# Placing the work around chunks 1 to 3 anew in a fused attention and maxout feed-forward kernel

## The chip, the cores and the metric

The kernel runs on one core of one Trainium2 chip. The core has a matrix engine (TensorE, PE in the profile, with its weight loads as PEld), a vector engine (VectorE, DVE), a scalar engine (ScalarE, ACT), a general engine (GpSimd, POOL) and a queue engine (SyncE, SP) that mostly issues transfers. Each engine runs its own list of instructions in order and waits on semaphores for the others. The metric is the device time of one execution, in microseconds (us).

## The reference: what is computed

Attention with a sliding window of 128 keys and 4 sink keys, for 4 batches of 8 heads, 768 positions and a head dimension of 64. Its result, taken as 3072 tokens of 512 features, then goes through a feed-forward layer whose hidden activation is the largest of three products.

```python
scores = scale * np.matmul(q, k.transpose(0, 1, 3, 2))
keep = is_sink | in_window            # first 4 keys, or 0 <= i - j < 128
a = softmax(np.where(keep, scores, -1e9))
x = np.matmul(a, v)                   # as [3072, 512]
h = np.maximum(np.maximum(x @ w1, x @ w2), x @ w3)   # [3072, 768]
out = h @ w_out                       # [3072, 512], float32
```

## The kernel before

**Tiling.** The 3072 tokens are cut into 12 chunks of 256 tokens, three to a batch (`ci // 3` is the batch, `ci % 3` the place in it). For each chunk the kernel makes these steps, each a small function:

- `load(ci, 'kqv')` issues the transfers of the raw float32 Q, K and V (SP's queue). A `gate` is a tiny POOL instruction that writes into the target first, so that the transfer waits for it.
- `cast_qk(ci, w, g, eng)` makes bf16 of half of Q or K (`g` is the group: head pairs 0 and 1, or 2 and 3), and `cast_v(ci, n, i, eng)` of a quarter of V, on the engine named.
- `turn(ci, w, g, eng)` brings the head dimension onto the partitions: four PE transposes into a PSUM bank, and a copy out of it by `eng`. From chunk 4 on `turn_dma` does that with a transposing transfer from SP's queue instead.
- `score(ci, (p,))` multiplies Q and K of head pair `p` (tile `st`, L331), `expo` takes the exponential on ACT (L398), and `mask` zeroes what is outside the window on DVE (L406). `sink_score` does it for the sink keys (tile `sk`).
- `av_open(ci)` takes four PSUM banks for the output of the four pairs (tile `o`) and, in chunks that have sinks apart, adds the sinks' share (L453). `av(ci, p)` adds the window's share (L471), then `norm` divides on DVE (L481 and L484, into `x_sb`).
- `xpose(ci, t, eng)` transposes a half of the result on PE and copies it into `xT`; from chunk 3 on `xpose_dma(ci)` does it with one transposing transfer (L503).
- `ffn_h(ci, fp, wi)` is one piece of the hidden layer: eight matmuls for a third of the columns (`fp`) with weight matrix `wi` (tile `h_ps`, L524). For `wi` = 0 ACT copies it to `h_sb` (L536); for 1 and 2 DVE takes the maximum into `h_sb` (L540). Nine pieces make a chunk.
- `ffn_y(ci, t)` is the output product for half of the tokens of a chunk: six matmuls (tile `y_ps`, L553), then a copy (L555).

**Order.** Nothing is scheduled by a tool: under `tc.manual_schedule()` every engine runs its instructions in the order in which the Python code calls them. So a line that is moved in the list at the end of the function moves its instructions on every engine that they touch. Chunks 0 to 3 are written out by hand, since the weights still arrive there; from chunk 4 on a loop repeats one order.

**Banks.** PSUM has eight banks, which `bank()` hands out by a first-in, first-out list, and `give()` puts back. A matmul into a bank waits until the instruction that last read the bank has finished. So the order of the calls also decides which earlier copy, exponential or maximum each matmul waits for.

**Buffers.** Raw Q, K and V have two buffers each (`bufs=2`), the turned tiles `qT`, `kT` and the V tiles `vb` a ring of four (`RING = 4`): chunk 4 uses the tiles of chunk 0. `kT_69` to `kT_72`, `qT_73` to `qT_76` and `vb_77` to `vb_80` are the ring's tiles 0 to 3 in the listings.

Of the kernel before, what the change touches and what calls it, by code (L numbers as in the profile page):

```python
# [16 lines left out]
def kernel(  # L17
# [13 lines left out]
    nc = tc.nc  # L31
# [17 lines left out]
    with tc.manual_schedule():  # L49
# [13 lines left out]
        def give(*banks):  # L63
            for x in banks:
                free.append(home.pop(id(x))[1])
# [46 lines left out]
        def cast_qk(ci, w, g, eng):  # L112

            if (ci, w) not in bfs:
                bfs[ci, w] = raw.tile([128, NP, 2, 2, D], BF16, tag=w + "_bf", name=w + "_bf")
            x, y = bfs[ci, w], raws[ci, w]
            f = eng.copy if eng is nc.scalar else eng.tensor_copy
            f(x[:, 2 * g:2 * g + 2].rearrange("q p i a d -> q p a i d"),  # L118
              y[:, 4 * g:4 * g + 4].rearrange("q (p a) i d -> q p a i d", a=2))

        def cast_v(ci, n, i, eng):
            if ci < NEW:
                eng.tensor_copy(  # L123
                    vb[ci % RING][64 * i:64 * i + 64, n, :, 0:D],
                    raws[ci, "v"][64 * n:64 * n + 64, :, i])
                return
            for h in range(2):
                x, y = 64 * h + 32 * i, 64 * n + 32 * h
                eng.tensor_copy(  # L129
                    vb[ci % RING][x:x + 32, n, :, 0:D], raws[ci, "v"][y:y + 32, :, i])  # L130
# [261 lines left out]
        def expo(ci, p):  # L392
            if ci >= NEW:
                return expo4(ci, p)
            lo = 0 if ci % CPB else 1
            e, st = es[ci, p]
            for a in range(2):
                nc.scalar.activation(e[:, a, lo:], st[a][:, lo:], AF.Exp, scale=scale)  # L398
                give(st[a])

        def mask(ci, p, eng=None):
            if ci >= NEW:
                return mask4(ci, p)
            lo = 0 if ci % CPB else 1
            e = es[ci, p][0]
            (eng or nc.vector).tensor_mul(e[:, :, lo:], e[:, :, lo:], msk0[0] if lo else msk)  # L406
# [38 lines left out]
        def av_open(ci):  # L445
            b, c = divmod(ci, CPB)
            for p in range(NP):
                os_[ci, p] = bank([128, 2, 2, D + 1], F32, "o")
            if c:
                for t in range(2):  # L450
                    for p in range(NP):
                        hp = slice(32 * p, 32 * p + 32)
                        nc.tensor.matmul(  # L453
                            os_[ci, p][:, t], lhsT=es[ci, "sink"][hp, t], rhs=vs[b % 2][hp],
                            start=(t == 0), stop=False, skip_group_check=True,
                            tile_position=(32 * p, 0))
# [54 lines left out]
        def ffn_h(ci, fp, wi, cuts=1, eng=nc.scalar, then=True):  # L511
            if ci not in hs:
                hs[ci] = work.tile([128, FB, 256], BF16, tag="h", bufs=3, name="h_sb")
            hp = bank([128, 2, 256], F32, "h_ps")
            for f in range(2):
                c0 = (2 * fp + f) * 128
                for ds in range(DS):
                    x = xTs[ci][:, ds]
                    if ci < NEW:
                        x = x.rearrange("q t (i r) -> q i t r", i=2)  # L520
                    else:
                        x = (x.rearrange("q t c -> q (t c)")
                             .rearrange("q (j i r) -> q i j r", i=2, r=32))
                    nc.tensor.matmul(  # L524
                        hp[:, f].rearrange("q (i t r) -> q i t r", i=2, r=x.shape[3]),
                        lhsT=w_sb[wi][:, ds, c0:c0 + 128], rhs=x,
                        start=(ds == 0), stop=(ds == DS - 1))
            maxima[ci, fp, wi] = hp
            if then:
                ffn_max(ci, fp, wi, cuts, eng)  # L530
# [14 lines left out]
        def ffn_y(ci, t, eng=None):  # L545
            if t == 0 and ci == 0:
                y01 = work.tile([128, 2, 2, d_model], F32, tag="y01", bufs=1, name="y01_sb")
                ys[0], ys[1], ys["01"] = y01[:, 0], y01[:, 1], y01
            if t == 0 and ci > 1:
                ys[ci] = work.tile([128, 2, d_model], F32, tag="y", bufs=5, name="y_sb")  # L550
            yp = bank([128, d_model], F32, "y_ps")
            for fb in range(FB):
                nc.tensor.matmul(yp, lhsT=hs[ci][:, fb, t * 128:(t + 1) * 128], rhs=wo[:, fb],  # L553
                                 start=(fb == 0), stop=(fb == FB - 1))
            (nc.scalar.copy if eng is None else eng.tensor_copy)(ys[ci][:, t], yp)  # L555
            give(yp)
# [197 lines left out]
        ffn_h(1, 1, 1)  # L754
        turn(2, 'k', 1, nc.scalar)
        cast_qk(2, 'q', 1, nc.scalar)
        cast_qk(2, 'q', 0, nc.vector)
        ffn_h(1, 2, 1)
        ffn_h(1, 1, 2)
        ffn_h(0, 0, 2)  # L760
        turn(2, 'q', 1, nc.scalar)
        ffn_h(0, 1, 2)
# [12 lines left out]
        cast_v(2, 1, 0, nc.gpsimd)  # L775
        cast_v(2, 0, 0, nc.gpsimd)
        ffn_h(0, 2, 2)
        ffn_h(1, 2, 2)
        score(2, (2,))
        cast_qk(3, 'q', 0, nc.gpsimd)  # L780
        av_open(2)
        mask(2, 1)
        expo(2, 2)
        cast_qk(3, 'k', 0, nc.gpsimd)
        load(4, 'v')
        mask(2, 3)
        mask(2, 2)
        cast_v(2, 1, 1, nc.vector)
        cast_v(2, 0, 1, nc.vector)
        cast_qk(3, 'q', 1, nc.vector)  # L790
        ffn_y(0, 0)
        ffn_y(0, 1)
        ffn_y(1, 0)
        av(2, 0)
        turn(3, 'q', 0, nc.scalar)
        cast_qk(3, 'k', 1, nc.scalar)
        load(5, 'q')
        av(2, 2)
        load(5, 'k', gate=after(0, 300))
        av(2, 3)  # L800
        turn(3, 'q', 1, nc.scalar)
        av(2, 1)
        turn(3, 'k', 1, nc.scalar)
        turn(3, 'k', 0, nc.scalar)
        ffn_y(1, 1)
        xpose(2, 0, nc.scalar)
        xpose(2, 1, nc.vector)
        cast_qk(4, 'q', 1, nc.vector)
        cast_v(3, 0, 0, nc.gpsimd)
        cast_v(3, 0, 1, nc.gpsimd)  # L810
        score(3, (1,))
        cast_v(3, 1, 1, nc.gpsimd)
        cast_qk(4, 'q', 0, nc.vector)
        expo(3, 1)
        score(3, (0,))
        cast_qk(4, 'k', 0, nc.vector)
        cast_qk(4, 'k', 1, nc.gpsimd)
        mask(3, 1)
        score(3, (3,))
        ffn_h(2, 0, 0)  # L820
        cast_v(4, 1, 0, nc.gpsimd)
        cast_v(3, 1, 0, nc.vector)
        turn_dma(4, 'k')
        turn_dma(4, 'q')
        expo(3, 0)
        expo(3, 3)
        score(3, (2,))
        ffn_h(2, 0, 2)
        mask(3, 0)
        mask(3, 3)  # L830
        ffn_h(2, 1, 0)
        ffn_h(2, 0, 1)
        expo(3, 2)
        av_open(3)
        mask(3, 2)
        av(3, 0)
        av(3, 1)
        ffn_h(2, 1, 1)
        av(3, 3)
        ffn_h(2, 2, 0)  # L840
# [158 lines left out]
```

## Time and profile before

| what | value |
|---|---|
| median of 3 runs | 177.17 us (176.39 to 177.6) |
| the profiled execution's own time | 176.99 us |
| its span, from first to last instruction | 175.3 us |
| PE busy | 168.9 us (96%) |
| DVE / POOL / ACT busy | 126.9 / 108.4 / 89.0 us |
| mean granted TensorE clock | 0.997 |
| from HBM / to HBM | 25.17 / 6.29 MB |

The span is 1.7 us shorter than the time of the same execution; the rest lies around it. Busy time of PE is modelled, and matmuls overlap: a PE that is shown busy can still be waiting inside a matmul, which is then seen as a longer distance from one start to the next. "[0.27 <-ACT k_bf L118]" behind a row says how long the engine sat idle before it, and what ended that. A piece of the chain of work that ended last reads "start, duration, what".

### The profile page before, as it was taken

The page shows a single profiled execution, that of the slowest core. Times are in us where ns is not written, and L with a number is a line of the kernel's source. Part 1 is how long each engine was busy: PE and PEld are TensorE (multiplying, and loading weights), DVE is VectorE, ACT ScalarE, POOL GpSimd, SP SyncE. Part 2 cuts the span into 40 slices and gives each one's busy share as a digit, 9 for nine tenths or more (in the row PEclk, how much of TensorE's full clock was granted, in tenths as well). Part 3 has the DMA queues.
Part 4 walks back from the last instruction along what each step waited for, and adds up shares of the span by engine and source line. Part 5 has one row for each costly group of instructions (what it writes and reads, how often), then busy time and mean ns, then how long its engine had stood idle before and what let it go on. Part 6 is the DMA issues. An engine that isn't in the chain of part 4 may idle for free.

```text
span 175.3 us, 5418 instructions
## 1 busy us (share of the span) xinstructions
PE 168.9 (96%) x2225; PEld 129.8 (74%) x2225; DVE 126.9 (72%) x264; ACT 89.0 (51%) x183; POOL 108.4 (62%) x191
## 2 busy tenths in 40 slices
PE   7979999999999999999999999999999999999992
PEld 2546899756687588698797797797797797796871
DVE  3177854799699797787976985986877777776452
ACT  4498654586863822925817717717726616510210
POOL 7389507244589999999999999789997700000000
PEclk9999999999999999999999999999999999999998
DMA  5999999999998997996999998998999509118303
GB/s 144 300 285 197 215 217 174 235 304 288 288 212 193 171 251 149 234 246 174 245 202 254 259 194 221 262 187 211 257 182 279 38 17 361 49 25 278 122 0 120
DMA packets 71545, 35.22 MB, mean 201 GB/s; under 512 B 27488, under 2 KB 69984, under 8 KB 71520
## 3 DMA queue, kind: packets, MB, share of 16 engines
q1 hardware_dynamic: 65824, 31.60, 76.9%
q0 software_dynamic: 5552, 3.15, 13.0%
q8 instruction: 17, 0.28, 0.7%
q10 hardware_dynamic: 144, 0.13, 0.2%
q14 instruction: 8, 0.07, 0.1%
HBM read 25.17 MB, written 6.29 MB: 179 GB/s over the span
## 4 chain that ended last, share of the span: by engine, by line
PE 87%; DVE 4%; ACT 3%; DMA 3%; issue 1%; ACTq 0%
PE h_ps L524 53%; PE y_ps L577 11%; PE o L471 6%; PE y_ps L553 5%; PE st L357 3%; PE warm L203 3%; DMA xT<-x_sb 3%; ACT e_sb L398 2%; PE pt L138 2%; PE st L331 1%; DVE vb L123 1%; PE o L453 1%; DVE x_sb L484 1%; PE y_ps L599 1%; PE sk L423 1%
## 5 line engine op out<-in xcount | busy, mean ns | idle before, releaser
L524 PE MATMUL h_ps<-xT,w 128*128 128x256 bf16 x864 | 101.2, 273 | 0.2
L524 PEld LDWEIGHTS <-w 128*128 128x128 bf16 x864 | 81.9, 98 | 10.3 <-DMA xT<-x_sb 0.5
L540 DVE TENSOR_TENSOR h_sb<-h_sb,h_ps 128x512 bf16<-128x512 bf16 (+1 forms) x74 | 49.0, 671 | 19.3 <-PE h_ps L524 15.6
L536 ACT CAST h_sb<-h_ps 128x512 bf16<-128x512 f32 x35 | 20.5, 586 | 52.6 <-PE h_ps L524 52.6
L129 POOL CAST vb<-v_raw 32x512 bf16<-32x512 f32 x48 | 37.0, 770 | 3.2 <-DMA v_raw<-in_v_dram 1.0
L90 POOL CAST k_bf<-k_raw 32x512 bf16<-32x512 f32 x48 | 29.1, 607 | 3.4 <-DMA k_raw<-in_k_dram 1.3
L398 ACT ACTIVATE e_sb<-st 128x512 bf16<-128x512 f32 (+1 forms) x48 | 23.1, 586 | 0.8 <-PE st L331 0.7
L484 DVE TENSOR_TENSOR x_sb<-o,rc 128x256 bf16<-128x256 f32 x48 | 20.4, 425 | 1.7
L577 PE MATMUL y_ps<-wo,h_sb 64*64 64x512 bf16 (+1 forms) x312 | 21.1, 377 | 0.0
L471 PE MATMUL o<-vb,e_sb 128*128 128x65 bf16 x352 | 16.8, 194 | 0.4 <-DVE vb L123 0.4
L471 PEld LDWEIGHTS <-e_sb 128*128 128x128 bf16 x352 | 14.6, 97 | 2.9 <-issue 0.8
L406 DVE TENSOR_TENSOR e_sb<-e_sb,msk 128x1024 bf16<-128x1024 bf16 (+1 forms) x18 | 15.3, 869 | 1.7 <-ACT e_sb L398 1.6
L123 POOL CAST vb<-v_raw 64x512 bf16<-64x512 f32 x16 | 11.4, 713 | 7.4 <-DMA v_raw<-in_v_dram 6.9
L389 DVE TENSOR_TENSOR e_sb<-e_part,msk 128x1024 bf16<-128x1024 bf16 x16 | 13.1, 831 | 3.3 <-ACT e_part L374 3.1
L577 PEld LDWEIGHTS <-h_sb 64*64 64x64 bf16 (+1 forms) x312 | 9.9, 106 | 5.0
L374 ACT ACTIVATE e_part<-st 128x384 bf16<-128x384 f32 x32 | 13.1, 496 | 0.5 <-PE st L357 0.5
L553 PE MATMUL y_ps<-wo,h_sb 128*128 128x512 bf16 x54 | 12.8, 380 | 0.0
L481 DVE RECIPROCAL rc<-o 128x4 f32<-128x4 f32 x48 | 8.4, 175 | 3.3 <-PE o L471 3.1
L118 POOL CAST k_bf<-k_raw 128x512 bf16<-128x512 f32 x6 | 4.1, 694 | 9.9 <-DMA k_raw<-in_k_dram 9.8
L553 PEld LDWEIGHTS <-h_sb 128*128 128x128 bf16 x54 | 4.9, 98 | 5.8 <-DVE h_sb L540 1.0
L118 ACT CAST q_bf<-q_raw 128x512 bf16<-128x512 f32 x13 | 7.6, 621 | 1.8 <-DMA q_raw<-in_q_dram 1.8
L427 ACT ACTIVATE e_sink<-sk 128x256 bf16<-128x256 f32 x8 | 3.1, 389 | 10.0 <-PE sk L423 10.0
(90 smaller groups left out, 145.1 us busy)
## 6 DMA issues: line engine op xcount, KB each, us to landing
k_raw<-in_k_dram SPq DMA_DIRECT2D x11, 512.0 KB, 5.3
v_raw<-in_v_dram SPq DMA_DIRECT2D x11, 512.0 KB, 5.7
q_raw<-in_q_dram SPq DMA_DIRECT2D x10, 512.0 KB, 6.7
out_dram<-y_sb SPq DMA_DIRECT2D x9, 512.0 KB, 3.1
w<-in_moe_w_dram POOLq DMA_DIRECT2D x9, 256.0 KB, 5.8
q_raw<-in_q_dram SPq DMA_DIRECT2D x4, 256.0 KB, 7.8
out_dram<-y_sb SPq DMA_DIRECT2D x1, 1024.0 KB, 5.2
wo<-in_moe_w_out_dram POOLq DMA_DIRECT2D x2, 384.0 KB, 6.1
```

The source lines that it names most:

```text
L90: f(bfs[ci, "k"][x:x + 32, :, n], raws[ci, "k"][y:y + 32, :, i].rearrange("q (p a) d -> q p a d", a=2))
L123: eng.tensor_copy(vb[ci % RING][64 * i:64 * i + 64, n, :, 0:D], raws[ci, "v"][64 * n:64 * n + 64, :, i])
L129: eng.tensor_copy(vb[ci % RING][x:x + 32, n, :, 0:D], raws[ci, "v"][y:y + 32, :, i])
L398: nc.scalar.activation(e[:, a, lo:], st[a][:, lo:], AF.Exp, scale=scale)
L406: (eng or nc.vector).tensor_mul(e[:, :, lo:], e[:, :, lo:], msk0[0] if lo else msk)
L471: nc.tensor.matmul(o[:, t, a], lhsT=e[:, a, s], rhs=vb[cv % RING][:, n, 2 * p + a], start=first, stop=True, skip_group_check=True)
L484: nc.vector.tensor_mul(xs[ci][:, p], o[:, :, :, 0:D], rc.unsqueeze(3).to_broadcast([128, 2, 2, D]))
L524: nc.tensor.matmul(hp[:, f].rearrange("q (i t r) -> q i t r", i=2, r=x.shape[3]), lhsT=w_sb[wi][:, ds, c0:c0 + 128], rhs=x, start=(ds == 0 ...
L536: (nc.scalar.copy if eng is nc.scalar else eng.tensor_copy)(dst, hp)
L540: nc.vector.tensor_max(dst[:, x], dst[:, x], hp[:, x])
L553: nc.tensor.matmul(yp, lhsT=hs[ci][:, fb, t * 128:(t + 1) * 128], rhs=wo[:, fb], start=(fb == 0), stop=(fb == FB - 1))
L577: nc.tensor.matmul(yps[ci][t][c:c + cols], lhsT=hs[ci][hp, fb, x:x + cols], rhs=wo[hp, fb], start=(turn == 0 and fb == 0), stop=(turn == 1 ...
```

## The change

No instruction is added or taken away. Calls are moved in the list for chunks 1 to 3, and some run on another engine: half of the Q cast of chunk 3 goes from DVE to ACT, and two of the four copies behind the transposes of chunk 3 go from ACT to DVE.

```diff
         ffn_h(1, 1, 1)
         turn(2, 'k', 1, nc.scalar)
         cast_qk(2, 'q', 1, nc.scalar)
-        cast_qk(2, 'q', 0, nc.vector)
         ffn_h(1, 2, 1)
         ffn_h(1, 1, 2)
+        cast_qk(2, 'q', 0, nc.vector)
         ffn_h(0, 0, 2)
...
         ffn_h(0, 2, 2)
-        ffn_h(1, 2, 2)
         score(2, (2,))
         cast_qk(3, 'q', 0, nc.gpsimd)
-        av_open(2)
         mask(2, 1)
+        cast_v(2, 0, 1, nc.vector)
+        cast_v(2, 1, 1, nc.vector)
         expo(2, 2)
         cast_qk(3, 'k', 0, nc.gpsimd)
         load(4, 'v')
         mask(2, 3)
         mask(2, 2)
-        cast_v(2, 1, 1, nc.vector)
-        cast_v(2, 0, 1, nc.vector)
-        cast_qk(3, 'q', 1, nc.vector)
         ffn_y(0, 0)
         ffn_y(0, 1)
-        ffn_y(1, 0)
+        cast_qk(3, 'q', 1, nc.scalar)
+        ffn_h(1, 2, 2)
+        av_open(2)
         av(2, 0)
-        turn(3, 'q', 0, nc.scalar)
+        av(2, 1)
         cast_qk(3, 'k', 1, nc.scalar)
         load(5, 'q')
-        av(2, 2)
         load(5, 'k', gate=after(0, 300))
         av(2, 3)
-        turn(3, 'q', 1, nc.scalar)
-        av(2, 1)
-        turn(3, 'k', 1, nc.scalar)
-        turn(3, 'k', 0, nc.scalar)
+        av(2, 2)
+        ffn_y(1, 0)
         ffn_y(1, 1)
         xpose(2, 0, nc.scalar)
         xpose(2, 1, nc.vector)
+        turn(3, 'q', 0, nc.scalar)
+        turn(3, 'k', 0, nc.scalar)
+        turn(3, 'q', 1, nc.vector)
+        turn(3, 'k', 1, nc.vector)
+        cast_v(3, 1, 0, nc.vector)
         cast_qk(4, 'q', 1, nc.vector)
         cast_v(3, 0, 0, nc.gpsimd)
         cast_v(3, 0, 1, nc.gpsimd)
+        ffn_h(2, 0, 0)
         score(3, (1,))
         cast_v(3, 1, 1, nc.gpsimd)
         cast_qk(4, 'q', 0, nc.vector)
         expo(3, 1)
         score(3, (0,))
-        cast_qk(4, 'k', 0, nc.vector)
         cast_qk(4, 'k', 1, nc.gpsimd)
         mask(3, 1)
+        ffn_h(2, 0, 2)
         score(3, (3,))
-        ffn_h(2, 0, 0)
+        score(3, (2,))
         cast_v(4, 1, 0, nc.gpsimd)
-        cast_v(3, 1, 0, nc.vector)
-        turn_dma(4, 'k')
         turn_dma(4, 'q')
         expo(3, 0)
         expo(3, 3)
-        score(3, (2,))
-        ffn_h(2, 0, 2)
         mask(3, 0)
+        cast_qk(4, 'k', 0, nc.vector)
         mask(3, 3)
+        turn_dma(4, 'k')
         ffn_h(2, 1, 0)
         ffn_h(2, 0, 1)
         expo(3, 2)
         av_open(3)
         mask(3, 2)
+        av(3, 1)
         av(3, 0)
-        av(3, 1)
         ffn_h(2, 1, 1)
```

Three places of the engines' own lists follow, where "-" is a row of before alone and "+" one of the change alone. The first is DVE from the turned K of chunk 2 (`kT_71`) to the V casts of chunk 2 (`vb_79`); `q_bf` is the Q cast of chunk 2, the L540 rows are maxima of `ffn_h`, the L406 rows are masks of chunk 2.

```order
 L149 COPY kT_71<-pt 128x2x256
+L540 TENSOR_TENSOR h_sb<-h_sb,h_ps 128x512 x3
+L118 CAST q_bf<-q_raw 128x2x2x2x64
+L540 TENSOR_TENSOR h_sb<-h_sb,h_ps 128x512 x3
+L406 TENSOR_TENSOR e_sb<-e_sb,msk 128x1024
 L540 TENSOR_TENSOR h_sb<-h_sb,h_ps 128x512
-L118 CAST q_bf<-q_raw 128x2x2x2x64
-L540 TENSOR_TENSOR h_sb<-h_sb,h_ps 128x512 x5
 L406 TENSOR_TENSOR e_sb<-e_sb,msk 128x1024
-L540 TENSOR_TENSOR h_sb<-h_sb,h_ps 128x512 x2
-L406 TENSOR_TENSOR e_sb<-e_sb,msk 128x1024 x3
 L123 CAST vb_79<-v_raw 64x8x64 x2
```

Between the copy of the turned K and the Q cast now stand three maxima instead of one, and behind the cast three instead of five. The two V casts have two of the chunk's masks ahead of them instead of four; the last two masks and the maximum of the kept-back `ffn_h(1, 2, 2)` come behind them.

The second place is DVE from the transposed result of chunk 2 (`xT`) into the masks of chunk 3 (`msk_0`); `qT_76` and `kT_72` are copies of the turned Q and K of chunk 3, `vb_80` a V cast of chunk 3, and the `q_bf` and `k_bf` casts belong to chunk 4.

```order
 L498 COPY xT<-xt 128x4x128
+L142 COPY qT_76<-pt 128x512
+L149 COPY kT_72<-pt 128x2x256
+L123 CAST vb_80<-v_raw 64x8x64
 L118 CAST q_bf<-q_raw 128x2x2x2x64 x2
+L406 TENSOR_TENSOR e_sb<-e_sb,msk_0_101 128x2x384
+L540 TENSOR_TENSOR h_sb<-h_sb,h_ps 128x512
+L406 TENSOR_TENSOR e_sb<-e_sb,msk_0_101 128x2x384
 L118 CAST k_bf<-k_raw 128x2x2x2x64
 L406 TENSOR_TENSOR e_sb<-e_sb,msk_0_101 128x2x384
-L123 CAST vb_80<-v_raw 64x8x64
-L540 TENSOR_TENSOR h_sb<-h_sb,h_ps 128x512
```

DVE takes two copies that ACT had, and the K cast of chunk 4 moved behind two masks and a maximum.

The third place is SP's queue after the loads for chunk 5, where `qT_73` and `kT_69` are the ring's tiles for chunk 4, the `v_raw` load is that of chunk 5 and `xT` the transposed result of chunk 3.

```order
 L107 DMA k_raw<-in_k_dram 128x8x128
+L188 DMA_TRANSPOSE qT_73<-q_bf 128x8x128
 L182 DMA_TRANSPOSE kT_69<-k_bf 128x8x64 x2
-L188 DMA_TRANSPOSE qT_73<-q_bf 128x8x128
 L107 DMA v_raw<-in_v_dram 128x8x128
 L503 DMA_TRANSPOSE xT<-x_sb 128x8x128
```

Q of chunk 4 is now turned ahead of K. On PE the order from the scores of chunk 2 on becomes: `score(2, 2)`, both halves of y of chunk 0, `ffn_h(1, 2, 2)`, the sinks' share and the four `av` of chunk 2, both halves of y of chunk 1, the transposes of chunk 2's result, all four transposes of chunk 3's Q and K, and then `ffn_h(2, 0, 0)` ahead of the scores of chunk 3. POOL's list is the same.

## The prediction

> **What bounds the kernel now.** The page comes first.
>
> ```profile
> PE 168.9 (96%) x2225; PEld 129.8 (74%) x2225; DVE 126.9 (72%) x264; ACT 89.0 (51%) x183; POOL 108.4 (62%) x191
> PE 87%; DVE 4%; ACT 3%; DMA 3%; issue 1%; ACTq 0%
> ```
>
> PE is the bound: it is busy for 168.9 of 175.3 us and holds 87% of the chain that ended last. The change takes no matmul away, so it can only win what PE loses in the stretch where calls move. The chain between 33 and 60 us shows where it leaves PE:
>
> ```profile
> 33.97 1.09 ACT e_sb L398 x2
> ...
> 35.33 1.97 ACT e_sb L398 x4
> ...
> 42.71 0.53 ACT k_bf L118
> ...
> 45.83 0.50 ACT xT L498
> ...
> 46.36 1.03 PE h_ps L524 x8
> ...
> 54.97 4.97 DMA xT<-x_sb
> ...
> 73.74 1.75 PE h_ps L524 x16
> ```
>
> The reader sees four places: exponentials at 34 to 37 us, a K cast at 42.7, the copy of the transposed chunk 2 at 45.8, and the transfer that transposes chunk 3, issued at 54.97 and landed at 59.94. What each costs PE is read from its timeline, from start to start. First the stretch concerned, then the same work further on, where nothing delays it:
>
> ```profile
> 33.48 1.05 PE L331 MATMUL st<-qT,kT 64*128 64x128 bf16 x18
> 34.46 0.29 PE L423 MATMUL sk<-qT,ks 128*32 128x256 bf16 x4
> 34.75 1.91 PE L524 MATMUL h_ps<-xT,w 128*128 128x256 bf16 x16
> ...
> 36.92 0.23 PE L453 MATMUL o<-vs,e_sink 32*128 32x130 bf16 x3
> 37.34 0.27 PE L453 MATMUL o<-vs,e_sink 32*128 32x130 bf16 x5 [0.19 <-ACT e_sb L398]
> 37.54 4.06 PE L553 MATMUL y_ps<-wo,h_sb 128*128 128x512 bf16 x18
> ...
> 42.61 0.40 PE L471 MATMUL o<-vb,e_sb 128*128 128x65 bf16 x8
> 43.29 0.62 PE L138 MATMUL pt<-ident,k_bf 128*128 128x128 bf16 x8 [0.27 <-ACT k_bf L118]
> ...
> 45.58 0.67 PE L331 MATMUL st<-qT,kT 64*128 64x256 bf16 x12
> ...
> 61.83 0.29 PE L453 MATMUL o<-vs,e_sink 32*128 32x130 bf16 x8
> 62.06 0.42 PE L471 MATMUL o<-vb,e_sb 128*128 128x65 bf16 x8
> 62.31 1.03 PE L524 MATMUL h_ps<-xT,w 128*128 128x256 bf16 x8
> ```
>
> **What the change removes.** (a) Scores of chunk 2, from 33.48 to 34.75: 1.27 us. The 22 matmuls show 1.05 and 0.29 us, pipeline overlap included; I take 1.0 as their undelayed distance, so 0.27 is lost. DVE's rows say why:
>
> ```profile
> 31.28 0.43 DVE L118 CAST q_bf<-q_raw 128x512 bf16<-128x512 f32 x1 [1.98 <-DMA q_raw<-in_q_dram]
> 31.62 3.07 DVE L540 TENSOR_TENSOR h_sb<-h_sb,h_ps 128x512 bf16<-128x512 bf16 x5
> ```
>
> The Q cast waits 1.98 us for its load with maxima queued behind it. Five of them then run from 31.62 to 34.69, and the scores and the next h piece need the banks that these read. With two maxima run inside the 1.98 us, the backlog goes; the last maximum then follows its own matmuls (about 33.7 to 34.4), ahead of need. The cast still starts at 31.28, when its data are there.
>
> (b) The sinks' share of chunk 2, from 36.92 to 37.54: 0.62, against 0.23 (61.83 to 62.06). Its banks wait for exponentials. In the change two y halves and the h piece stand ahead of it: 18 y matmuls in 4.06 make 1.3 to 1.35 a half, an h piece shows 0.9 to 1.0, so PE comes there at 39.35. The last four exponentials end by then: four took 1.97 to 37.3, and two more at that pace end at 38.3. Saved: 0.39.
>
> (c) From the last `av` to the K transposes: 42.61 to 43.29 is 0.68, against 0.25 (62.06 to 62.31). All four turns now come two y halves and a transpose later, about 1.5 us after the last of their casts. Saved: 0.43.
>
> (d) `ffn_h(2, 0, 0)` at 46.36 follows ACT's copy of `xT`. The scores ahead of it start at 45.58 and show 0.67, of which 0.05 to 0.1 is overlap, so 0.1 to 0.2 of the 0.78 us to the piece is lost; I take 0.17. In the change the four turns (sixteen transposes; eight show 0.62) stand between the transposed result and the piece. Adding up, PE ends them at 44.5, and the copies of `xT` end at 44.2 on DVE and 44.4 on ACT. Saved: 0.17, with a cover of 0.1.
>
> Together 1.26 us: by `ffn_h(2, 1, 0)` PE is at 47.25 where it was at 48.5.
>
> **What it adds or makes late.** The new y of chunk 0 needs the last maximum of its h: its matmuls reach it at 36.7, DVE ends it at 36.5. That costs nothing. ACT's casts of chunk 3 now stand ahead of the y copies of chunk 1, and the K half waits for its load; POOL shows when that lands:
>
> ```profile
> 41.38 0.90 POOL L118 CAST k_bf<-k_raw 128x512 bf16<-128x512 f32 x1 [1.48 <-DMA k_raw<-in_k_dram]
> 37.26 1.63 POOL L123 CAST vb<-v_raw 64x512 bf16<-64x512 f32 x2 [4.79 <-DMA v_raw<-in_v_dram]
> 37.30 3.15 DVE L406 TENSOR_TENSOR e_sb<-e_sb,msk 128x1024 bf16<-128x1024 bf16 x3
> ```
>
> So ACT casts until about 42.0, and the first y copy is due at 42.06: nothing, and one for one with a later load. The V casts ahead of the masks wait for V, which lands as POOL's row starts, at 37.2. Two casts end at 38.1, two masks of 1.05 at 40.2, and the fourth `av` wants the last mask at 40.3. Cover 0.1; I take nothing, and 0.3 at worst, if each of the two casts loses part of one of POOL's (0.8 each by its row).
>
> Here a rule of the Trainium skill speaks against the change. POOL's V casts run from 37.26 to 38.89, just when DVE's would now; before, DVE's stood at 40.5, when POOL was idle. In "SBUF — State Buffer", section "Who interferes with whom", it says that DVE casts in a two-port mode, and DVE operations with two SBUF inputs against a reading POOL, exclude POOL for a whole instruction, the loser blocking. This trace agrees in part: a mask takes 1.05 beside POOL. By the rule the two V casts would each wait for a POOL cast, and the masks would end some 0.3 us later, which would make the gain 1.0 instead of 1.26.
>
> Then DVE becomes the engine to watch:
>
> ```profile
> 46.70 0.42 DVE L118 CAST k_bf<-k_raw 128x512 bf16<-128x512 f32 x1
> 47.12 0.87 DVE L406 TENSOR_TENSOR e_sb<-e_sb,msk 128x768 bf16<-128x768 bf16 x1
> 49.36 1.68 DVE L406 TENSOR_TENSOR e_sb<-e_sb,msk 128x768 bf16<-128x768 bf16 x2
> 51.56 0.54 DVE L406 TENSOR_TENSOR e_sb<-e_sb,msk 128x768 bf16<-128x768 bf16 x1
> 52.03 0.17 DVE L481 RECIPROCAL rc<-o 128x4 f32<-128x4 f32 x1
> 50.00:55.00 5.00, 5.00 (x65) 4.48 (x64) 4.86 (x14) 1.51 (x4) 4.78 (x10) 1.00 1.10 170
> ```
>
> From 50 to 55 us it is busy for 4.86 of 5.0. In the change it takes two copies from ACT, done by 45.2, then three casts of 0.4 until 46.3, and waits for the first exponentials of chunk 3: ACT copies the piece that PE ends at 45.4 and makes two of them, to 46.95. First mask to 47.8, maximum of `ffn_h(2, 0, 2)` to 48.45. Now `ffn_h(2, 0, 1)` needs that very bank, while PE is there at 48.15: **a new wait** of 0.3 at the slow mask (0.87), none at the fast one (0.54). I take 0.2. Mask, K cast of chunk 4, mask, maximum and mask follow, and the first reciprocal comes at 51.1 to 51.6, where it was at 52.03: DVE gains 0.4 to 0.9, less than PE.
>
> The same list sets SP's queue:
>
> ```profile
> 47.61 3.09 SPq L182 DMA_TRANSPOSE kT<-k_bf  x2
> 50.75 1.30 SPq L188 DMA_TRANSPOSE qT<-q_bf  x1
> 52.15 0.53 SPq L107 DMA_DIRECT2D v_raw<-in_v_dram  x1
> 54.97 1.24 SPq L503 DMA_TRANSPOSE xT<-x_sb  x1
> 66.95 1.77 SPq L503 DMA_TRANSPOSE xT<-x_sb  x1
> DMA to landing us min/median/max: 3.1/3.1/5.0
> DMA to landing us min/median/max: 3.2/4.0/5.2
> 55.53 0.28 PE L423 MATMUL sk<-qT,ks 128*32 128x256 bf16 x4
> ```
>
> (The two landing rows are those of L503 and of L182.) Q of chunk 4 can go at 46.4, when the load ahead has been issued. K's two transposes wait for the K cast, which moves from 46.7 to 49.0: issue 49.5 to 52.6, 1.9 later than before. The V load behind them goes at 52.7 instead of 52.15. The transpose of chunk 3 waits for the last quotient, and so gains DVE's 0.4 to 0.9: issue at 54.1 to 54.6. At the same 4.97 to landing it lands at 59.0 to 59.5. At the median of 3.1 it would be 57.3, but the V load in front has come closer, so I take the long one. PE, 1.05 ahead, wants it at 58.9, or at 59.2 with a small wait on the way. **Term at the end:** `ffn_h(3, 0, 0)` starts at about 59.35 instead of 59.98. Sum: -1.26 + 0.2 (bank) + 0.4 (transfer) = -0.66 us.
>
> Behind 60 us the code is the same, and PE has no gaps as long as those; the next transpose of this kind is issued at 66.95, lands some 3 us later, and its h pieces stand at 73.74 in the chain, so a shift of half a microsecond has room to carry to the end. The profiled execution took 176.99; less 0.66 that is 176.3. The median of the runs shown, 177.17, would give 176.5. I say **176.4**.
>
> **The rivals.**
> 1. *All of it arrives.* The landing is as fast as the median allows and the mask is the fast one: 1.26 less 0.1 for the V casts, so 175.8. For it: only one in nine of these transfers took 5 us. Against: the V load moves right in front of it, and DVE is full.
> 2. *Nothing arrives.* The V load, 0.5 later, holds the transpose back until 59.9 as before: 177.0. For it: at 54.97 the transfer took 4.97 because something was in front of it, and that something moves later.
> 3. *Slower: K of chunk 4 is late.* The K cast behind two masks delays K's transposes, and everything behind them on SP. With 3.2 to 4.0 us to landing the second lands at 54.3 to 55.1, and PE wants it at 54.7, just behind the sinks' scores (55.53 before); ahead it had 3 us of cover. From a cast later than about 49.3 each us costs one, in the scores and again in the V load and the transpose behind it. A K cast at 50.5 would move those by 1.4: the transpose lands at 61, 1.1 later than before, so 178.1.
> 4. *It does not do what it says.* If a load sets DVE's and ACT's pace (V at 37.2 and K at 41.4 have hardly any cover), the waits only change their names and the time stays at 177.0; this counts with the second.
>
> **Chances.** Forecast (0.3 to 0.95 gained) 0.48; all of it 0.17; nothing (within 0.3) 0.21; slower by K 0.14. The range takes the bounds of the rivals, 175.6 at the quickest and 178.0, where the K cast is 1.1 us late. One per cent, 1.8 us, is about what a measurement of this kernel can tell from no change. A gain of that size is more than all four waits hold: 0.04. A loss of it needs K at 51: 0.08. So within 1%: 0.88.
>
> **What would show it.** Right: no idle time on PE between 33 and 47 us; the Q cast still at 31.3; `ffn_h(2, 1, 0)` at 47.3; the K cast of chunk 4 near 49; xT of chunk 3 issued near 54.3 and PE waiting for it. Wrong: PE idle before the fourth `av`, before `ffn_h(2, 0, 0)`, or before the first scores of chunk 4.

## The result and the profile after

| kernel | median | runs | ratio to the kernel before, 95% interval |
|---|---|---|---|
| before | 176.83 us (176.25 to 178.34) | 22 | |
| the change | 177.62 us (176.72 to 178.46) | 22 | 1.0037 [1.0019, 1.0055] |

The change is slower by 0.4%, some 0.65 us; 0.66 us faster was forecast. The profiled execution of the change took 177.06 us (span 175.3), hardly more than that of before (176.99), so it is a quick one of its kind. The experiments below include a second one.

The first two rows are those of the page after, busy times and the shares of the chain; the others are pieces of its chain (start, duration, what):

```profile
PE 167.7 (96%) x2220; PEld 129.1 (74%) x2225; DVE 127.9 (73%) x265; ACT 88.3 (50%) x182; POOL 108.6 (62%) x191
PE 69%; DMA 16%; POOL 6%; DVE 4%; issue 2%; ACT 0%; POOLq 0%; SPq 0%; ACTq 0%
...
30.85 6.73 DMA v_raw<-in_v_dram
...
38.80 2.01 DVE e_sb L406 x2
...
50.15 0.88 DVE e_sb L406
51.68 1.03 PE h_ps L524 x8
...
54.95 5.05 DMA xT<-x_sb
60.05 1.92 PE h_ps L524 x16
```

ACT, which held the chain four times before, holds hardly anything of it (0.6 us of exponentials around 47 us). In its place stand the load of V of chunk 2 with two masks behind it, a mask at 50, and again the transpose of chunk 3, landed at 60.00. The 16% of DMA are mostly two transfers of the front part, over by 30.52 us, where the two kernels are still the same. `ffn_h(3, 0, 0)` starts at 60.05, against 59.98. PE's timeline of the change, for the four waits that were to go:

```profile
33.12 0.84 PE L331 MATMUL st<-qT,kT 64*128 64x128 bf16 x18
33.89 0.29 PE L423 MATMUL sk<-qT,ks 128*32 128x256 bf16 x4
34.11 1.05 PE L524 MATMUL h_ps<-xT,w 128*128 128x256 bf16 x8
...
38.99 0.29 PE L453 MATMUL o<-vs,e_sink 32*128 32x130 bf16 x8
39.21 1.05 PE L471 MATMUL o<-vb,e_sb 128*128 128x65 bf16 x24
40.86 0.41 PE L471 MATMUL o<-vb,e_sb 128*128 128x65 bf16 x8 [0.60 <-DVE e_sb L406]
...
45.04 1.04 PE L524 MATMUL h_ps<-xT,w 128*128 128x256 bf16 x8
...
47.86 0.94 PE L524 MATMUL h_ps<-xT,w 128*128 128x256 bf16 x7
...
51.68 1.03 PE L524 MATMUL h_ps<-xT,w 128*128 128x256 bf16 x8 [0.23 <-DVE h_sb L540]
```

The scores of chunk 2 take 0.99 us to the next piece (33.12 to 34.11; 1.27 before), the sinks' share 0.22 (0.62 before), and the first h piece of chunk 2 has no wait. New are 0.60 us ahead of the fourth `av`. At 47.86, `ffn_h(2, 1, 0)`, PE is 0.63 us ahead of before (48.49). At 51.68, `ffn_h(2, 2, 0)`, nothing is left: 51.69 before. DVE's rows of that stretch:

```profile
37.60 1.18 DVE L123 CAST vb<-v_raw 64x512 bf16<-64x512 f32 x2 [0.92 <-DMA v_raw<-in_v_dram]
38.80 2.00 DVE L406 TENSOR_TENSOR e_sb<-e_sb,msk 128x1024 bf16<-128x1024 bf16 x2
...
47.51 0.56 DVE L406 TENSOR_TENSOR e_sb<-e_sb,msk 128x768 bf16<-128x768 bf16 x1 [0.49 <-ACT e_sb L398]
47.98 0.68 DVE L540 TENSOR_TENSOR h_sb<-h_sb,h_ps 128x512 bf16<-128x512 bf16 x1
48.58 0.82 DVE L406 TENSOR_TENSOR e_sb<-e_sb,msk 128x768 bf16<-128x768 bf16 x1
49.32 0.83 DVE L118 CAST k_bf<-k_raw 128x512 bf16<-128x512 f32 x1
50.07 0.96 DVE L406 TENSOR_TENSOR e_sb<-e_sb,msk 128x768 bf16<-128x768 bf16 x1
50.95 0.67 DVE L540 TENSOR_TENSOR h_sb<-h_sb,h_ps 128x512 bf16<-128x512 bf16 x1
...
52.02 0.17 DVE L481 RECIPROCAL rc<-o 128x4 f32<-128x4 f32 x1
```

V of chunk 2 lands at 37.58 here and DVE waits 0.92 us for it. Later the K cast of chunk 4 takes 0.83 us, twice its 0.42 of before, because POOL is already casting when it starts (49.08 to 51.50), and the masks around it take 0.82 and 0.96. So the maximum on which `ffn_h(2, 2, 0)` waits ends at 51.63, and the first reciprocal starts at 52.02 (52.03 before). SP's rows:

```profile
47.09 3.07 SPq L188 DMA_TRANSPOSE qT<-q_bf  x1
50.26 2.53 SPq L182 DMA_TRANSPOSE kT<-k_bf  x2
52.88 0.54 SPq L107 DMA_DIRECT2D v_raw<-in_v_dram  x1
54.95 1.24 SPq L503 DMA_TRANSPOSE xT<-x_sb  x1
```

The V load of chunk 5 leaves at 52.88 instead of 52.15, and lands at 58.97 instead of 56.82: 6.09 us instead of 4.66. What happens on the DMA engines meanwhile is seen in 40 slices of 0.1 us from 56 to 60 us: the bytes moved, and the packets of the queue that brings instructions (count, MB, and their time as a share of 16 engines' 4 us).

```profile
GB/s 348 358 310 264 282 463 228 133 64 18 33 44 51 123 133 61 56 46 23 5 15 8 10 8 10 8 10 10 10 215 289 300 283 348 343 358 282 246 312 297
...
q8 instruction: 1, 0.02, 2.3%
```

And the packets of the window from 57 to 59 us alone:

```profile
DMA packets 344, 0.09 MB, mean 44 GB/s; under 512 B 344, under 2 KB 344, under 8 KB 344
```

From 57.8 to 58.9 us the 16 engines together move about 10 GB/s, though the transpose of chunk 3 has been issued since 54.95. One packet of the instruction queue is under way at that time: 2.3% of 64 us is 1.5 us, in the trace from 56.56 to 58.05. The load's 512 KB come in 1024 packets of 512 bytes, and the last of them ends at 56.70; from 57 to 59 us there is none. What is late of the load is its report: it counts as landed when 16 parts have reported, and of these 5 come by 57.4 and 11 at 58.92 to 58.97. The transpose's 256 KB come in 1024 packets of 256 bytes, from 56.22 to 59.29, and 17 of them start at 57.4, take 1.5 us each and end at 58.91 to 58.95. So it is the transpose's own packets that are held up here, with an instruction packet among them. The load in front cost little in this execution: the transpose's first packet came 1.27 us after its issue, against 1.16 to 1.18 where nothing was in the way.

**What sets the start of `ffn_h(3, 0, 0)`.** Ahead of it PE does the second y half of chunk 2, six matmuls that take 1.31 us where nothing follows late. What the distance from the start of that half to the start of the piece has over 1.31 is PE's wait for the transpose of chunk 3: in every profile where there is a wait, the piece starts 0.04 or 0.05 us behind the landing. And 117.0 us behind this start the execution ends, in before, after and the fastest kernel alike (176.99 - 59.98, 177.06 - 60.05, 175.57 - 58.56; in a_pad it is 117.3). So this one place tells what a kernel has won. From the profiles:

| run | V load issued, landed | transpose issued, landed | second y half | `ffn_h(3,0,0)` | PE's wait | ratio, all runs |
|---|---|---|---|---|---|---|
| before | 52.15, 56.82 | 54.97, 59.94 | 58.46 | 59.98 | 0.21 | 1 |
| the change | 52.88, 58.97 | 54.95, 60.00 | 58.44 | 60.05 | 0.30 | 1.0037 |
| after_2 (the change again) | 53.20, 59.20 | 54.83, 60.25 | 58.32 | 60.30 | 0.67 | 1.0023 |
| a_k_early | 52.42, 56.70 | 53.89, 59.63 | 57.38 | 59.68 | 0.99 | 0.9984 |
| a_k_cast | 52.27, 58.37 | 54.00, 59.41 | 57.49 | 59.46 | 0.66 | 1.0031 |
| b_k_late | 53.56, 60.00 | 55.68, 61.06 | 59.17 | 61.10 | 0.62 | 1.0064 |
| b_qk_order | 52.82, 58.64 | 54.60, 59.66 | 58.09 | 59.71 | 0.31 | 1.0007 |
| a_xt_first | 55.09, 60.20 | 53.76, 56.93 | 57.26 | 58.56 | 0 | 0.9937 |
| a_xt_first_2 | 55.79, 61.20 | 54.47, 59.25 | 57.96 | 59.30 | 0.03 | 0.9952 |
| a_xt_k | 55.06, 60.36 | 53.73, 58.70 | 57.26 | 58.74 | 0.17 | 0.9946 |
| a_pad | 53.04, 58.13 | 54.45, 59.14 | 57.84 | 59.19 | 0.04 | 0.9959 |
| a_pad_half | 53.48, 58.85 | 54.62, 59.86 | 58.12 | 59.91 | 0.48 | 1.0010 |
| b_pad | 53.23, 58.31 | 55.79, 59.33 | 59.29 | 60.59 | 0 | 1.0032 |

A profile is one execution, and its front part comes up to a microsecond earlier or later by chance; the ratios are from all runs. Before, the transpose came only 0.21 us after PE was ready for it. A PE that comes a microsecond earlier meets a transpose that doesn't.

### The profile page after: what moved, and what is told of

Read it like the earlier page. It is cut to its first block, busy times and chain, and to the rows that moved or that the text cites. A ratio compares the mean times of both kernels' runs of the same rounds, so it can differ in the third digit from the quotient of the medians.

```text
span 175.3 us, 5420 instructions
## 1 busy us (share of the span) xinstructions
PE 167.7 (96%) x2220; PEld 129.1 (74%) x2225; DVE 127.9 (73%) x265; ACT 88.3 (50%) x182; POOL 108.6 (62%) x191
## 4 chain that ended last, share of the span: by engine, by line
PE 69%; DMA 16%; POOL 6%; DVE 4%; issue 2%; ACT 0%; POOLq 0%; SPq 0%; ACTq 0%
PE h_ps L524 43%; PE y_ps L577 11%; DMA v_raw<-in_v_dram 7%; DMA w<-in_moe_w_dram 7%; PE o L471 5%; PE y_ps L553 4%; PE st L357 3%; POOL w L292 3%; DMA xT<-x_sb 3%; DVE e_sb L406 2%; POOL vb L123 1%; PE st L331 1%; PE o L453 1%; PE y_ps L599 1%; DVE vb L123 1%
## 5 line engine op out<-in xcount | busy, mean ns | idle before, releaser
L540 DVE TENSOR_TENSOR h_sb<-h_sb,h_ps 128x512 bf16<-128x512 bf16 (+1 forms) x74 | 49.3, 670 | 19.9 <-PE h_ps L524 16.1
L129 POOL CAST vb<-v_raw 32x512 bf16<-32x512 f32 x48 | 37.3, 777 | 3.0 <-PE h_ps L524 0.4
L406 DVE TENSOR_TENSOR e_sb<-e_sb,msk 128x1024 bf16<-128x1024 bf16 (+1 forms) x18 | 14.3, 808 | 2.7 <-ACT e_sb L398 2.5
L389 DVE TENSOR_TENSOR e_sb<-e_part,msk 128x1024 bf16<-128x1024 bf16 x16 | 13.7, 881 | 3.1 <-ACT e_part L374 2.9
L118 ACT CAST q_bf<-q_raw 128x512 bf16<-128x512 f32 x14 | 8.2, 620 | 2.9 <-DMA q_raw<-in_q_dram 2.8
```

Source lines behind the costliest of these rows:

```text
L129: eng.tensor_copy(vb[ci % RING][x:x + 32, n, :, 0:D], raws[ci, "v"][y:y + 32, :, i])
L540: nc.vector.tensor_max(dst[:, x], dst[:, x], hp[:, x])
```

## Experiments

**V casts of chunk 2.** Is it the wait for V, which DVE now meets ahead of two masks? The change with the casts one mask later:

```diff
         mask(2, 1)
-        cast_v(2, 0, 1, nc.vector)
-        cast_v(2, 1, 1, nc.vector)
         ...
         mask(2, 3)
+        cast_v(2, 0, 1, nc.vector)
+        cast_v(2, 1, 1, nc.vector)
         mask(2, 2)
```

> The change, with DVE's two V casts of chunk 2 one mask later (behind the mask of pair 3, ahead of that of pair 2). Theory V (the V casts wait 0.92 us for their load with two masks behind them, and the last av waits 0.76 us for the last mask): DVE's wait shrinks to 0.3 us or less, the last av of chunk 2 waits 0.1 us or less, and the time comes down by 0.5 to 0.8 us from the change's 177.6, to the time of before or a little under. Theory K (the later K cast of chunk 4 delays everything behind it on SP) and theory X (the transpose of chunk 3 is held by the V load in front of it): the av wait goes, but the transpose of chunk 3 lands as before and the time stays within 0.2 us of the change's.

Measured: 176.98 us, ratio 1.0002 [0.9967, 1.0037]. And the casts alone, put ahead of the last two masks in the kernel before:

> The kernel before, with DVE's V casts of chunk 2 ahead of the last two masks, as in the change, and nothing else. Theory V: DVE idles about 0.1 to 0.9 us for the load, but three y halves stand between the masks and the av, so at most 0.2 us arrives: within 0.3 us of before. The same part costs only where the y halves no longer cover it. If the part alone costs 0.5 us or more, it is DVE's lost time and not the av wait that matters. Theories K and X: the time of before.

Measured: 176.82 us, 1.0002 [0.9973, 1.0031]. Alone they cost nothing that can be measured; in the change the interval is too wide to tell. In the profile of a_v_mid PE has no wait at the `av`, and `ffn_h(3, 0, 0)` still starts at 59.81, 0.04 us behind a transpose that landed at 59.77. The change itself, a second time:

> The change once more, unaltered, beside the next three on one chip, for a second trace of it. Theory X (the transpose of chunk 3 lands near 59.7 us whenever it is issued between 53.9 and 55.1, because the V load of chunk 5 is in front of it): the first h piece of chunk 3 starts at 59.7 us or later, right at the landing. Theory K (the late K cast and the exchanged transposes push the V load, and with it that landing, later): the V load is issued near 52.9 us, lands at 58.5 or later, and the time is 0.4 to 0.8 us above before. Theory V (late V of chunk 2): the last av of chunk 2 waits 0.5 us or more in this trace too; if it waits less and the time is still above before, V is not the cause.

Measured: 177.19 us, 1.0023 [1.0005, 1.0041]. In this profile V landed at 37.29, DVE waited 0.19 instead of 0.92 us for it, and `ffn_h(3, 0, 0)` still started at 60.30. V of chunk 2 is not what takes the gain.

**K of chunk 4.** The change with its cast and its transposes where they stood before:

```diff
+        cast_qk(4, 'k', 0, nc.vector)
         cast_qk(4, 'k', 1, nc.gpsimd)
         ...
+        turn_dma(4, 'k')
         turn_dma(4, 'q')
         ...
         mask(3, 0)
-        cast_qk(4, 'k', 0, nc.vector)
         mask(3, 3)
-        turn_dma(4, 'k')
```

> The change, with the K cast of chunk 4 back ahead of the first mask of chunk 3 and K of chunk 4 turned ahead of Q again. Theory K: K's transposes are issued 2 us earlier, the V load of chunk 5 too, the transpose of chunk 3 lands 0.5 us or more earlier, and the time comes down by 0.5 to 0.8 us. Theory V: the av wait of 0.76 us stays, and the time is within 0.2 us of the change's. Theory X: the V load goes 0.5 us earlier and the time comes down by 0.2 to 0.5.

Measured: 176.63 us, 0.9984 [0.9952, 1.0016]. The gain on DVE comes back, and is lost again at the transpose. PE's timeline of that run:

```profile
50.67 1.04 PE L524 MATMUL h_ps<-xT,w 128*128 128x256 bf16 x8
...
57.38 1.47 PE L553 MATMUL y_ps<-wo,h_sb 128*128 128x512 bf16 x6
59.68 0.50 PE L524 MATMUL h_ps<-xT,w 128*128 128x256 bf16 x3 [0.83 <-DMA xT<-x_sb]
```

`ffn_h(2, 2, 0)` starts at 50.67 without a wait, 1.0 us ahead of before; then PE stands 0.83 us for a transpose that took 5.74 us. The reverse, the kernel before with only K's cast and transposes where the change has them:

> The kernel before, with only the chunk 4 part of the change: the K cast behind a mask of chunk 3, and Q turned ahead of K. Theory K: the V load of chunk 5 is issued 0.5 us or more later, the transpose of chunk 3 lands 0.5 to 1 us later, and the time is 0.5 to 0.9 us above before. Theories X and V without K: within 0.2 us of before.

Measured: 177.99 us, 1.0064 [1.0041, 1.0087], the slowest of all. DVE's rows of it:

```profile
50.04 0.83 DVE L118 CAST k_bf<-k_raw 128x512 bf16<-128x512 f32 x1
50.80 0.95 DVE L406 TENSOR_TENSOR e_sb<-e_sb,msk 128x768 bf16<-128x768 bf16 x1
51.67 0.68 DVE L540 TENSOR_TENSOR h_sb<-h_sb,h_ps 128x512 bf16<-128x512 bf16 x1
```

The cast takes 0.83 here too (0.42 in the profile of before), and everything behind it is 0.7 us late: the maximum starts at 51.67 instead of 50.97. The rule from the Trainium skill that the prediction weighed for the V casts ("SBUF — State Buffer", "Who interferes with whom") bears on this cast instead; it agrees with the row, with DVE as the loser. Who loses went by who started first, not by the place of the cast: before, DVE's started at 46.70 and POOL's at 46.74, and POOL's took 0.84 us instead of 0.61; in a_k_early, in the old place, POOL's started at 46.29 and DVE's at 46.43, and DVE's took 0.84. The two halves of the move apart, first the change with only the cast put back (K still turned behind Q), then the kernel before with only Q turned ahead of K:

> The change with DVE's K cast of chunk 4 put back ahead of the first mask of chunk 3, but K still turned behind Q. If DVE's chain (mask, K cast, mask, maximum) is what gives the gain back: ratio near 0.998, as with cast and turn both put back (0.9984), and `ffn_h(2,2,0)` at 50.9 instead of 51.6 us. If it is SyncE's order, in which K's transposes stand behind Q's and hold the V load: ratio 1.002, with `ffn_h(2,2,0)` early, and the transpose of chunk 3 landing at 60 all the same.

Measured: 177.19 us, 1.0031 [1.0009, 1.0053], though `ffn_h(2, 2, 0)` started at 50.81 in its profile. So an earlier DVE alone wins nothing.

> The kernel before with only Q of chunk 4 turned ahead of K, the casts where they were. If DVE's late K cast alone made the 0.64% of the earlier run in which both were moved: no difference here, 0.999 to 1.001. If the order of the transposes in SyncE's queue made it: 1.003 to 1.006, with K landing after 53 us and the V load of chunk 5 leaving after 52.7.

Measured: 176.76 us, 1.0007 [0.9989, 1.0025], although K landed at 54.35 and the V load left at 52.82 and took 5.8 us. The order alone costs little or nothing in the kernel before: PE is ready for the transpose only at 59.40 there (58.09 and 1.31), and waits 0.31 us for it, against 0.21. The two expectations, held side by side, contradict each other: by the first the order counts, by the second it doesn't. Cast and order are no two terms to be added: an earlier DVE brings nothing where the transpose is late, and a late load costs nothing where PE is late.

**The V load of chunk 5, behind the transpose.**

```diff
-        load(5, 'v', gate=pool_gate)
         xpose_dma(3)
+        load(5, 'v', gate=pool_gate)
```

> The change, with the V load of chunk 5 issued behind the transpose of chunk 3 instead of in front of it. Theory X: the transpose lands in about 3 us instead of 5, PE does not wait at the first h piece of chunk 3, and the time comes down by 0.3 to 0.8 us. Theories V and K: PE is there no more than 0.2 us before the transpose lands, so the time comes down by 0.2 us at most.

Measured: 175.66 us, 0.9937 [0.9904, 0.9970]; a second time, on another chip:

> The change with the V load of chunk 5 issued behind the transpose of chunk 3, a second time, beside the three below. If TensorE's wait for that transpose is what takes the gain: ratio 0.993 to 0.997, `ffn_h(3,0,0)` before 59.3 us of the profile, the transpose landing under 4 us from its issue. If the first run of this kernel was fast because DVE's masks of chunk 3 happened to fall between POOL's casts (0.55 us each there, 0.82 and 0.96 in the change): ratio 0.998 to 1.002 when they take 0.8 us or more this time.

Measured: 175.84 us, 0.9952 [0.9931, 0.9973], with slow masks this time (0.92 and 0.96 us), so that lucky masks alone aren't the reason. They did cost this execution 0.7 us: from `ffn_h(2, 1, 0)` to `ffn_h(2, 2, 0)` it took 3.92 us, 3.20 before. Its transpose took 4.78 us and not under 4 as expected, and PE hardly waited because it came late itself. The chain of the first of them:

```profile
51.72 2.62 PE h_ps L524 x24
...
57.33 1.40 PE y_ps L553 x6
58.73 1.75 PE h_ps L524 x16
```

From 16 us on no transfer stands in the chain, and PE goes from one row to the next without a wait (the first matmul of the piece starts at 58.56; the last group of the chain begins a little behind it). The same move in the kernel before:

> The kernel before, with the V load of chunk 5 issued behind the transpose of chunk 3. Theory X: PE stood ready for chunk 3 at most 0.2 us ahead of the landing, so the time comes down by 0.0 to 0.3 us only: before, the four waits on PE set the time, and the transfer hid behind them. If it comes down by 0.8 us or more, as the same exchange did in the changed kernel, the other parts of the change are worth nothing by themselves.

Measured: 176.64 us, 0.9995 [0.9975, 1.0014]. There PE was ready only 0.21 us ahead of the transpose, so that 0.1% was all that could be won. The line needs the removed waits to pay. Together with the two moves tried above, first with the V casts and K, then with K alone:

> The change with three undone or amended parts together: V load of chunk 5 behind the transpose of chunk 3, V casts of chunk 2 one mask later, K cast and transposes of chunk 4 as before. If the wait for the transpose is the only thing in the way (theory X), it is no faster than with the exchange of the V load alone (175.7 us). If the late K of chunk 4 or V of chunk 2 cost something beside it, it is 0.2 to 0.5 us faster.

Measured: 176.02 us, 0.9967 [0.9941, 0.9993], no faster than with the V load alone moved.

> The change with the V load of chunk 5 behind the transpose of chunk 3 and with the K cast of chunk 4 where it stood before, K turned ahead of Q. If the late K cast and the load in front of the transpose each take a part of the gain, the parts do not overlap, and this is the fastest of all: ratio 0.991 to 0.995. If they are one and the same delay seen twice, it is as fast as with the V load alone moved, 0.993 to 0.997. If the K cast only shifts work that DVE has spare time for, the same.

Measured: 175.76 us, 0.9946 [0.9927, 0.9966], the same as with the V load alone moved (0.9952 on the same chip). K's place, worth 0.4 to 0.5% with the load in front of the transpose (0.9984 against 1.0023 and 1.0037, on different chips), is worth nothing measurable with it behind. That points to K mattering through the transfers, but the first difference is hardly clear of its intervals. And the DMA row of that run, 40 slices of 0.1 us from 56 to 60 us:

```profile
GB/s 108 172 144 126 110 366 87 77 56 51 61 61 77 189 282 302 287 292 348 338 333 323 348 353 343 328 333 348 353 338 333 348 302 312 266 302 297 282 292 297
```

The transpose's packets run from 54.89 to 56.58 here, though it lands, by its last report, only at 58.70. The load's follow from 56.27 to 58.71, some 300 GB/s from 57.4 on. The instruction packet is under way from 56.58 to 57.45, just behind the transpose's last packet; in the change it came among them.

**The instruction packet.** What makes load and transpose land late? Packets of 16 KB on the instruction queue come about every 10 us. If the one at 56.5 to 58 us holds the load, moving it must help. Seven long matmuls of the warm-up at the start are replaced by 46 short ones, which puts 78 more instructions into PE's list (39 matmuls with their weight loads) and touches nothing else:

```diff
+                for _ in range(more):
+                    nc.tensor.matmul(pw[:, 0:64], lhsT=wz[:, 0:128], rhs=wz[:, 0:64], start=True, stop=True)
...
-        warm(8)
+        warm(4, 24)
...
-        warm(4)
+        warm(1, 22)
```

> The change, with 7 of the 12 long matmuls of the warm-up (512 columns) replaced by 46 short ones (64 columns): 39 more matmuls, 78 more instructions of TensorE ahead of everything, so that the instruction packet now at 56.6 to 57.4 us comes near 53.5 to 54.5. If the packet holds the V load and the transpose of chunk 3: V lands 4.7 us after its issue or sooner, the transpose 3.2 to 4 after its own, no hole of 10 GB/s at 57 to 59 us, `ffn_h(3,0,0)` at 59.2 to 59.6, ratio 0.994 to 0.998. If the later V load alone counts: landing 59.5 to 60.3 and ratio 1.001 to 1.005 as before.

Measured: 176.16 us, 0.9959 [0.9943, 0.9975]. The packet came at 52.89. The DMA rows of this run, 40 slices of 0.1 us, first from 52 to 56, with the instruction queue, then from 56 to 60 us:

```profile
GB/s 292 287 287 282 265 287 292 292 357 41 100 120 113 138 154 148 156 136 100 26 8 8 10 10 10 8 10 18 0 0 72 61 128 82 82 133 82 41 77 143
...
q8 instruction: 1, 0.02, 1.7%
```

```profile
GB/s 154 261 307 348 323 338 343 348 348 353 338 338 335 307 300 294 264 220 113 87 284 289 287 292 301 264 215 261 220 251 256 317 328 333 323 343 328 323 323 317
```

The hole of 10 GB/s has moved with the packet, from 58 to 54 us, where K's transposes are under way with time to spare; at 58 us the engines move some 300 GB/s. The V load takes 5.1 us instead of 6.1, the transpose 4.7 instead of 5.0 to 5.4, and PE waits 0.04 us for it. The same with 19 more matmuls:

> The change, with 3 of the long warm-up matmuls replaced by 22 short ones: 19 more matmuls, the packet about 1.5 us earlier, near 55 to 56 us, still while the V load is under way. If the packet holds the transfers it holds the V load here for a while but is over by 56.5 to 57: the transpose lands at 59 or before, ratio 0.996 to 1.000. If the packet doesn't count: 1.001 to 1.005.

Measured: 177.01 us, 1.0010 [0.9988, 1.0032]. The packet came at 56.21, only 0.4 to 1.2 us earlier than in the change, the hole stayed (57.9 to 58.6 us), and the transpose took 5.24. By the ratio the packet would not count, but it was not moved out of the way either, so this run tells nothing apart. And the 39 in the kernel before:

> The kernel before with the same 39 more short matmuls in the warm-up. Its transpose of chunk 3 landed at 59.94 after 4.97 us, with TensorE hardly waiting for it. If the packet holds it: it lands about 1 us sooner, but TensorE is there no earlier than 59.8, so ratio 0.998 to 1.000. If the packet doesn't count: 0.999 to 1.001. Both would give a larger number, the same for the change, if the short matmuls delay the start.

Measured: 177.25 us, 1.0032 [1.0002, 1.0062], slower, which neither theory expected. Its packet came at 54.8 and its transpose took only 3.54 us, as the theory says, but that run was late from the start: its chain shows where.

```profile
31.80 6.72 DMA v_raw<-in_v_dram
...
40.10 7.84 DMA k_raw<-in_k_dram
```

Two loads of the front part hold PE, which they didn't before. Packets of 16 KB now stand at 31.6 and 44.9 us instead of 37.3 and 47.9. That they hold these loads is likely, but was not tried.

All 17 profiles together say more than these three runs. Some of them, by the packet records of the trace (the transpose's 1024 packets, and the one of the instruction queue nearest to them):

| run | instruction packet | transpose issued | its packets | they took |
|---|---|---|---|---|
| before | 57.64 to 58.58 | 54.97 | 56.14 to 58.88 | 2.7 |
| the change | 56.56 to 58.05 | 54.95 | 56.22 to 59.29 | 3.1 |
| a_k_early | 56.71 to 58.10 | 53.89 | 55.74 to 58.77 | 3.0 |
| a_xt_first_2 | 56.99 to 57.96 | 54.47 | 55.63 to 58.45 | 2.8 |
| a_xt_first | 56.43 to 57.43 | 53.76 | 54.93 to 56.45 | 1.5 |
| a_xt_k | 56.58 to 57.45 | 53.73 | 54.89 to 56.58 | 1.7 |
| a_pad | 52.89 to 53.96 | 54.45 | 57.16 to 58.52 | 1.4 |
| b_pad | 54.82 to 55.78 | 55.79 | 56.97 to 58.77 | 1.8 |

In the five profiles with no instruction packet among them (a_xt_v_k is the fifth) the transpose's packets took 1.4 to 1.8 us, in the other twelve 2.4 to 3.5. So the packet stretches the transpose itself, in the kernel before too. The load in front sets when the transpose can begin: in a_k_early 1.85 us after its issue and in a_pad 2.7, in both some 0.45 us before the load's last packet ended, and 1.16 to 1.18 us after it with the load behind.

## Why the prediction was wrong

1. **The four waits**: right. (a), (b), (c) and (d) are gone from the profile. From the first scores of chunk 2 to `ffn_h(2, 1, 0)` PE took 15.01 us before (33.48 to 48.49) and 14.02, 13.90 and 14.11 in after_2, a_xt_first and a_xt_first_2: 0.9 to 1.1 us are won there, 1.26 were forecast. Without the wait for the transpose the gain arrives: by all runs the kernel gains 0.8 to 1.1 us on before (0.9952 and 0.9937).
2. **V casts ahead of masks, "I take nothing, and 0.3 at worst"**: by all runs nothing (1.0002 alone). In one execution a late V costs more, 0.60 us of PE's time in the profile after, since the casts stand ahead of two masks. PE idle before the fourth `av` was one of the prediction's own signs of being wrong.
3. **The new wait of 0.2 at `ffn_h(2, 0, 1)`**: at another place, and larger. PE came later than I had it there, and waited for DVE at the `av` ahead of `ffn_h(2, 2, 0)` and at that piece, 0.6 us together: from `ffn_h(2, 1, 1)` to it took 1.70 us (49.98 to 51.68), 1.09 before (50.60 to 51.69).
4. **"DVE gains 0.4 to 0.9"**: the first step that failed. In both profiles of the change DVE gained 0.0 and 0.1 (reciprocal at 52.02 and 51.89). The K cast was taken at its old 0.42 us; behind a POOL cast it took 0.83, and the masks around it were slow ones (0.82 to 0.98). In these two executions that took 0.6 and 0.8 us of PE's lead, more than the transpose did, and the transpose was issued at 54.95 and 54.83 instead of 54.1 to 54.6. In a_xt_first the masks took 0.55 and DVE did gain, so this step varies from one execution to the next.
5. **"Term at the end", 4.97 us from issue to landing**: the second step that failed, and enough alone. I took the longest landing seen as the bound, and moved it with the issue. But where DVE did gain (a_k_early, a_k_cast), the transpose, issued at 53.89 and 54.00, landed at 59.63 and 59.41: 5.74 and 5.41 us. It begins only when the load in front is nearly through, and then its packets take 2.4 to 3.5 us instead of 1.4 to 1.8 when an instruction packet comes among them. The sum held the landing fixed, with no term for the end of the load or for a packet. That the profile after shows 5.05, so near to 4.97, is luck. Without the packet (a_pad) the transpose landed at 59.14, inside the 59.0 to 59.5 forecast.
6. **Rival 2** had the right transfer and half of the mechanism: the V load in front does hold the start of the transpose, but not in the kernel before, where its first packet came 1.17 us after its issue and the instruction packet made the 4.97. It gave 177.0, since it took the landing of before as the latest. **Rival 3** had K of chunk 4 late by its cast. The scores of chunk 4 didn't wait for K, but what stands behind it on SP was late.

Shown are: that with the V load ahead of the transpose the change gains nothing, and with it behind the gain comes (a_xt_first, twice, beside b_xt_first); and that moving the instruction packets away recovers most of it (a_pad). That K's place counts only through the transfers (a_xt_k beside a_xt_first_2) is likely, not shown. Open is the full size. In the two profiles of the change the piece starts 0.07 and 0.32 us later than before, while the medians on the same chips are 0.8 and 0.4 us apart, and moving the V load is worth 1.3 to 1.8 us by the ratios (0.9937 and 0.9952 against 1.0023 and 1.0037, of 177 us), about twice PE's longest wait in these two profiles. So the usual execution must wait longer than the profiled ones, as that of a_k_early does (0.99); no profile shows it, nor how much of it is DVE's. And a_pad moves all packets, not that one alone.

## What to carry to other kernels

Before a wait on an engine is removed, look for the transfer that the same engine meets next, and ask what stands ahead of it in its queue. A transfer that lands just in time may be set by the load in front of it, or by a packet of the instruction queue, and then an earlier issue brings little. Here one exchanged line (the load behind the transpose, which had time) turned the change from 0.4% slower into 0.5% faster than before.

## What was not expected of the hardware

- **Instruction fetch is seen in the data transfers.** A single 16 KB packet of the instruction queue took 0.9 to 1.6 us on its way. Where it came among the packets of the transpose, these took 2.4 to 3.5 us instead of 1.4 to 1.8, and in most such profiles the 16 engines fell to about 10 GB/s for 0.5 to 1.5 us. 39 short matmuls at the start were worth 0.7% to the change (0.9959 against 1.0023 to 1.0037) and cost the kernel before 0.3%. The Trainium skill ("Runtime: NRT & Kernel Launch", "Instruction fetch mechanics") says that a block has 16 KiB, 256 instructions, and that the cost of crossing one is "mostly hidden". The size agrees with the packets here; for the transfers beside it the cost was not hidden.
- **A transpose behind a load in its queue begins when the load is nearly through, not when it has landed.** In the change the load's last packet ended at 56.70 and its last report came at 58.97, while the transpose's packets ran from 56.22. With the load behind, the transpose of chunk 3 landed at 56.93 to 59.25 in the changed kernel, and the load, 5.1 to 5.4 us after its issue, cost nobody anything.
- **The same cast on DVE costs 0.42 or 0.83 us**, by whether a POOL cast was under way when it started.
